# A's queries projected transposed in a gated mix of linear and sliding-window attention on one core: denominators beside the numerators, heads copied by ScalarE and normalised by GpSimd, gate logits on TensorE

## The chip, the cores and the metric

One core of a Trainium2 chip runs the kernel. The metric is device time in microseconds (us), the median of three runs. The core has five engines with a queue of instructions each: TensorE (PE, its weight loads are listed as PEld), VectorE (DVE), ScalarE (ACT), GpSimd (POOL) and SyncE (SP), which issues most DMAs. Matmul results lie in PSUM, the other tiles in SBUF.

## What is computed

Both attentions share the input x of 2048 rows and 1024 columns; there are 32 heads of 32 columns.

```python
def _A_ref(x, wqkv, wo):
    q, k, v = ...                                   # x @ wqkv, split into 32 heads of 32
    phi = lambda t: jnp.where(t > 0, t + 1, jnp.exp(t)) + 1e-6
    pq, pk = phi(q), phi(k)
    kv = jnp.einsum("bhsd,bhse->bhde", pk, v)
    z = jnp.einsum("bhsd->bhd", pk)
    num = jnp.einsum("bhqd,bhde->bhqe", pq, kv)
    den = jnp.einsum("bhqd,bhd->bhq", pq, z)[..., None] + 1e-6
    return merge_heads(num / den) @ wo
def _B_ref(x, wqkv, wo):
    W, dil = 8, 2                                   # a query sees itself and 7 keys, 2 apart
    ...
    attn = _softmax(jnp.where(mask, logits * Dh ** -0.5, -1e9))
    return merge_heads(jnp.einsum("bhsw,bhswd->bhsd", attn, vg)) @ wo
g = _sigmoid((x * gate_w).sum(-1, keepdims=True))
return g * _A_ref(...) + (1 - g) * _B_ref(...)
```

The kernel writes g as e/(1+e) with e = exp(logit) and 1−g as 1/(1+e). So A's normalised heads are multiplied by e, both outputs go into one sum in PSUM, and that sum is multiplied by 1/(1+e) (the tile `omg`; e is `el`).

## The kernel before

**Tiles.** Because the window steps by two, even and odd rows of x never meet in B. The kernel splits them into two parities p of 1024 rows, each of eight tiles of 128 rows; a *pair* is a tile and the one four further on in the same parity. x lies transposed in SBUF (xT), columns on partitions.

**Projections.** A `Group` makes a 2×2 block of 128×512 (or, for column groups, 512-row) results with seven products instead of eight (m1 to m7, a Strassen form), four 128×512 matmuls each. For this, sums of x (`xsums`) and of the weights (`Weights.sums`) are made beforehand. Products accumulate in four PSUM banks X0, Y0, X1, Y1. Three intermediate results per group are copied out by ACT (`save`, L266); of the four final blocks one is written by ACT (L237) and three are added by DVE (L239). The last products m3 and m4 of a group run inside the next group. A *row group* has rows of x on partitions of its result, a *column group* has weight columns there, so that its result is transposed.

**Attention as filler.** After each product `side(rate)` draws steps from a queue of generators: score steps and numerator steps of B, and the KV sums of A. B works on items (four heads of each half, nn = 0 to 3, times parity p); each has ten score steps (L513, then exp on ACT L520 and the mask on DVE L522) and nine numerator steps (L532). A numerator step makes 114 rows of eight heads with 33 columns, the last of which is the softmax denominator, since V carries a column of ones. DVE takes its reciprocal (L535) and multiplies straight out of PSUM (L537), and SP stores the tile (L542) in OB_d.

**Stages.** x and B's value weights are loaded and transposed; the first two pairs are projected in the plain way; `xsums` of all pairs; B's values for pairs 2 to 7 (a DRAM tensor V_d); B's keys and queries nn = 0; `gate` for 16 tiles (x rows loaded again, a DVE multiply-and-reduce L227, exp on ACT); A's keys and values as row groups, with phi (ACT L397, DVE L398 and L399), the sum of phi(k) on GpSimd (L418) and KV on PE (L437); B's nn = 1 lies between them and nn = 2, 3 around A's queries. A's queries are row groups (`qa_group`): phi, then per tile GpSimd multiplies by the sum of phi(k) (L486), DVE reduces over each head (L488), L491 to L493 turn this into e/den, GpSimd scales (L495) and SP stores PQ_d (L496). Meanwhile `kv_end` multiplies KV into A's output weights (L465). At the end 16 output tiles: two transposing DMAs each (L651, L653) and 32 matmuls (L659, L661).

**Order.** Every engine works its queue in order, and a scheduler has fixed that order when the kernel was built. Pools (`bufs`) decide when a tile is free for the next writer. SP carries all loads and stores of the middle and the end in one queue.

Of the kernel before, what the change touches and what calls it, by code (L numbers as in the profile page):

```python
# [14 lines left out]
P = 128  # L15
QB = 114
NBLK = 9
EPS = 1e-6


@with_exitstack
def kernel(
# [31 lines left out]
    PQ_d = [dram.tile([P, D], BF16, name=f"PQ_d{t}") for t in range(16)]  # L54

    chainp = ctx.enter_context(tc.tile_pool(name="chainp", bufs=5))
    tring = ctx.enter_context(tc.tile_pool(name="tring", bufs=4))
    ering = ctx.enter_context(tc.tile_pool(name="ering", bufs=4))
    smallp = ctx.enter_context(tc.tile_pool(name="smallp", bufs=4))
    obp = ctx.enter_context(tc.tile_pool(name="obp", bufs=4))  # L60
# [6 lines left out]
    ph1 = ExitStack()  # L67
    xp = ph1.enter_context(tc.tile_pool(name="xp", bufs=1))
    kqp = ph1.enter_context(tc.tile_pool(name="kqp", bufs=2))
    vwp = ph1.enter_context(tc.tile_pool(name="vwp", bufs=2))  # L70
    ptp = ph1.enter_context(tc.tile_pool(name="ptp", bufs=1))
    prodp = ph1.enter_context(tc.tile_pool(name="prodp", bufs=2))
# [7 lines left out]
    S4 = xp.tile([P, 4, 2, 512], FP16, name="S4")  # L80

# [5 lines left out]
    def xsums(p, c0, c1):  # L87
        sl = slice(c0 * P, c1 * P)
# [3 lines left out]
        s3 = xT.bitcast(FP16)[:, 0:4, p, 1, sl]  # L92
        tt = nc.vector.tensor_tensor
        tt(out=s1, in0=a21, in1=a22, op=ALU.add)
        tt(out=s2, in0=s1, in1=a11, op=ALU.subtract)
        tt(out=s3, in0=a11, in1=a21, op=ALU.subtract)
        tt(out=s4, in0=a12, in1=s2, op=ALU.subtract)

    class XOp:


        def get(self, m, kc, p, sl):
            if m == 1:
                return xT[:, kc, p, 0, sl]
            if m == 2:
                return xT[:, 4 + kc, p, 0, sl]
            if m == 4:
                return xT[:, 4 + kc, p, 1, sl]
            if m == 7:
                return xT.bitcast(FP16)[:, kc, p, 1, sl]  # L110
            return {3: S4, 5: S1, 6: S2}[m][:, kc, p, sl]

    xop = XOp()

    class Weights:

        def __init__(self, n, W, T, eng, parts=1):
            self.n, self.W, self.T, self.eng = n, W, T, eng  # L120
            self.W16 = W.bitcast(FP16)

        def sums(self, lo=0, hi=4):
            n, W, T, tt = self.n, self.W, self.T, self.eng.tensor_tensor
            b11, b12 = W[:, lo:hi, 0:n], W[:, lo:hi, n:2 * n]
            b21, b22 = W[:, 4 + lo:4 + hi, 0:n], W[:, 4 + lo:4 + hi, n:2 * n]
            t3 = self.W16[:, lo:hi, n:2 * n]
            t1, t2, t4 = T[:, 0, lo:hi, :], T[:, 1, lo:hi, :], T[:, 2, lo:hi, :]
            tt(out=t1, in0=b12, in1=b11, op=ALU.subtract)
            tt(out=t3, in0=b22, in1=b12, op=ALU.subtract)  # L130
            tt(out=t2, in0=b22, in1=t1, op=ALU.subtract)
            tt(out=t4, in0=b21, in1=t2, op=ALU.subtract)

        def get(self, m, kc, sl):
            n = self.n
            lo, hi = sl.start, sl.stop
            if m == 1:
                return self.W[:, kc, lo:hi]
            if m == 2:
                return self.W[:, 4 + kc, lo:hi]  # L140
            if m == 3:
                return self.W[:, 4 + kc, n + lo:n + hi]
            if m == 7:
                return self.W16[:, kc, n + lo:n + hi]
            return self.T[:, {5: 0, 6: 1, 4: 2}[m], kc, lo:hi]

    def row_weights(src, col0, eng, dq, quarters=True):
# [3 lines left out]
        for j in range(2):  # L151
            for i in range(2):
                dq.dma_start(out=W[:, 4 * i:4 * i + 4, 512 * j:512 * j + 512],
                             in_=view[:, 4 * i:4 * i + 4, col0 + 512 * j:col0 + 512 * j + 512])
        return Weights(512, W, T, eng)

    def col_weights(src, col0, nn, eng, dq):
# [3 lines left out]
        for j in range(2):  # L161
            c0 = col0 + 512 * j + nn * P
            dq.dma_start(out=W[:, :, j * P:(j + 1) * P], in_=view[:, :, c0:c0 + P])
        return Weights(P, W, T, eng)
# [4 lines left out]
    wvB = None  # L169
    xt_load(0)  # L170
    W = wp.tile([P, 8, D], BF16, name="W", tag="W")
    T = tp.tile([P, 3, 4, 512], FP16, name="T", tag="T")
    bview = B_wqkv.rearrange("(k p) n -> p k n", p=P)

    def vb_load(dq, i, j):
        dq.dma_start(out=W[:, 4 * i:4 * i + 4, 512 * j:512 * j + 512],
                     in_=bview[:, 4 * i:4 * i + 4, 2 * D + 512 * j:2 * D + 512 * j + 512])
    vb_load(nc.scalar, 0, 0)
    vb_load(nc.scalar, 1, 0)
    xt_load(4)  # L180
    vb_load(nc.scalar, 0, 1)
    vb_load(nc.scalar, 1, 1)
    for t in (1, 5, 2, 6, 3, 7):
        xt_load(t)
    wvB = Weights(512, W, T, nc.vector)
    for t in (8, 12, 9, 13, 10, 14, 11, 15):
        xt_load(t)
# [15 lines left out]
    bd = consts.tile([P, P], F32, name="bd")  # L203
    nc.gpsimd.memset(bd[:], 0.0)
    for i in range(4):
        nc.gpsimd.memset(bd[32 * i:32 * i + 32, 32 * i:32 * i + 32], 1.0)
    ones = consts.tile([P, P], F32, name="ones")
    nc.gpsimd.memset(ones[:], 1.0)
    gw_row = prodp.tile([P, D], BF16, name="gw_row", tag="prod")
    nc.sync.dma_start(out=gw_row[:], in_=gate_w.partition_broadcast(P))  # L210
    el = consts.tile([P, 16], F32, name="el")
    omg = consts.tile([P, 16], F32, name="omg")
    zacc = consts.tile([P, D], F32, name="zacc")
    KVacc = consts.tile([P, D], F32, name="KVacc")
    KVb = consts.tile([P, 8, P], BF16, name="KVb")
# [5 lines left out]

    def gate(t):
        xt = tring.tile([P, D], BF16, name="xrow", tag="t")
        nc.sync.dma_start(out=xt[:], in_=xrows(t))
        junk = ering.tile([P, D], BF16, name="gjunk", tag="e")
        dot = smallp.tile([P, 1], F32, name="gdot", tag="gdot")
        nc.vector.tensor_tensor_reduce(out=junk[:], in0=xt[:], in1=gw_row[:], scale=1.0, scalar=0.0,  # L227
                                       op0=ALU.mult, op1=ALU.add, accum_out=dot[:])
        nc.scalar.activation(out=el[:, t:t + 1], in_=dot[:], func=ACT.Exp)
        nc.vector.tensor_scalar(out=omg[:, t:t + 1], in0=el[:, t:t + 1], scalar1=1.0, scalar2=None,  # L230
                                op0=ALU.add)
        nc.vector.reciprocal(out=omg[:, t:t + 1], in_=omg[:, t:t + 1])
# [10 lines left out]
    class Group:  # L243
# [3 lines left out]
        def __init__(self, final, done=None):  # L247
            self.final, self.done = final, done
# [3 lines left out]
        def operands(self, m, kc):  # L252
            raise NotImplementedError

        def mm(self, ps, m, start, stop):
            for kc in range(4):
                lhsT, rhs = self.operands(m, kc)
                nc.tensor.matmul(ps[:], lhsT=lhsT, rhs=rhs, start=start and kc == 0,  # L258
# [439 lines left out]
```

## Time and profile before

| quantity | value |
|---|---|
| median of three runs | 604.92 us (603.25 to 605.2) |
| the profiled execution, as timed | 605.71 us |
| its span in the trace | 603.9 us |
| instructions in the trace | 8465 |
| DMA | 56.15 MB, mean 93 GB/s |

The profile gives busy time per engine, a chain of waits from the last instruction back to the first, groups of instructions by source line (`out<-in`, with the partitions and elements), and stretches of the span with the busy time of each engine. The granted clock is TensorE's, 1.0 at full speed. An engine that waits is idle, and what ended the idle time is named behind an arrow. The lines themselves are shown in the prediction.

### The profile page before, as it was taken

What the parts mean: (1) busy time and instruction counts of PE and PEld (TensorE: products, weight loads), DVE (VectorE), ACT (ScalarE), POOL (GpSimd) and SP (SyncE); (2) the same over time, 40 slices, a digit from 0 to 9 for tenths busy, and PEclk for the clock granted to TensorE, in tenths of its full rate; (3) what the DMA queues carried; (4) which work ended last, traced back from release to release, by engine and by line L of the source; (5) the groups of instructions that cost most, each with busy time, mean ns of one, the idle gap of its engine ahead of it and who ended that gap; (6) DMA issues with size and microseconds to landing.
All of it is one profiled execution on the core that took longest, in us unless ns stands there. A gap on an engine that the chain in (4) does not pass through costs nothing.

```text
span 603.9 us, 8465 instructions
## 1 busy us (share of the span) xinstructions
PE 504.1 (83%) x3140; PEld 234.5 (39%) x3194; DVE 371.3 (61%) x648; ACT 225.3 (37%) x347; POOL 215.1 (36%) x156
## 2 busy tenths in 40 slices
PE   7769985889999998979979765694986389999997
PEld 4324431334444444434444322242332244444443
DVE  1643469999777568878454988858488964001100
ACT  1313332455553465525644542254353143100000
POOL 6059348453222056222816775314056500000000
PEclk9969996979999999989979986595797769999999
DMA  9997481700200240027403121103108366554311
GB/s 232 174 246 213 134 264 49 186 22 13 49 9 11 48 88 9 13 49 238 154 21 74 46 68 43 52 8 95 51 14 183 100 133 139 124 114 112 63 44 35
DMA packets 126057, 56.15 MB, mean 93 GB/s; under 512 B 105408, under 2 KB 117696, under 8 KB 126016
## 3 DMA queue, kind: packets, MB, share of 16 engines
q1 hardware_dynamic: 123904, 53.51, 35.9%
q10 hardware_dynamic: 2112, 2.10, 1.2%
q8 instruction: 25, 0.41, 0.3%
q14 instruction: 16, 0.13, 0.1%
HBM read 26.10 MB, written 16.91 MB: 71 GB/s over the span
## 4 chain that ended last, share of the span: by engine, by line
PE 48%; DVE 29%; issue 5%; POOL 5%; ACT 3%; DMA 3%; SPq 0%; another core or an unknown queue 0%; DVEq 0%; ACTq 0%
PE X L258 14%; PE Y L258 12%; PE po L661 9%; PE po L659 8%; DVE eA L399 6%; DVE PT L522 5%; POOL prod L486 4%; DVE gjunk L227 4%; DVE tA L239 2%; DVE tA L398 2%; DVE den L488 2%; PE s L513 2%; ACT PT L520 2%; DMA xrow<-in_A_x_dram 2%; DVE ob L537 1%
## 5 line engine op out<-in xcount | busy, mean ns | idle before, releaser
L520 ACT ACTIVATE PT<-s 128x912 bf16<-128x912 f32 (+1 forms) x80 | 68.6, 857 | 61.5 <-PE o L532 32.4
L522 DVE TENSOR_TENSOR PT<-PT,maskp 128x912 bf16<-128x912 bf16 (+1 forms) x80 | 65.9, 828 | 20.3 <-ACT PT L520 20.0
L258 PEld LDWEIGHTS <-xT 128*128 128x128 bf16 (+1 forms) x480 | 46.0, 100 | 78.6 <-issue 33.6
L258 PE MATMUL Y<-W,xT 128*128 128x512 f16 (+1 forms) x233 | 63.4, 394 | 14.7 <-DVE va L239 9.9
L258 PE MATMUL X<-T,S 128*128 128x512 f16 x240 | 63.8, 388 | 1.3 <-ACT M1s L266 0.8
L659 PE MATMUL po<-WoA,pqT 128*128 128x512 bf16 x249 | 61.8, 388 | 3.4 <-DMA pqT<-PQ_d 2.9
L486 POOL TENSOR_TENSOR prod<-eA,zacc 128x512 f32<-128x512 bf16 x32 | 41.0, 1304 | 64.5 <-DVE eA L399 51.0
L661 PE MATMUL po<-WoB,obT 128*128 128x512 bf16 x249 | 62.6, 386 | 1.5 <-DMA obT<-OB_d 1.1
L665 DVE TENSOR_SCALAR osb<-po,omg 128x512 bf16<-128x512 f32 x16 | 12.0, 750 | 82.5 <-PE po L661 82.4
L418 POOL TENSOR_TENSOR zacc<-zacc,eA 128x1024 f32<-128x1024 f32 x15 | 33.6, 2239 | 69.4 <-DVE eA L399 46.2
L266 ACT COPY U4s<-X 128x512 f32<-128x512 f32 x46 | 26.9, 585 | 78.9 <-PE X L258 76.9
L532 PE MATMUL o<-vw,PT 128*128 128x33 bf16 x576 | 30.1, 184 | 28.4 <-DVE PT L522 21.2
L399 DVE SCALAR_TENSOR_TENSOR eA<-eA,tA 128x1024 bf16<-128x1024 bf16 x32 | 52.4, 1637 | 0.6
L258 PEld LDWEIGHTS <-S 128*128 128x128 f16 x360 | 33.7, 99 | 41.3 <-issue 4.9
L258 PE MATMUL Y<-xT,WS 128*128 128x512 f16 (+1 forms) x124 | 39.9, 450 | 8.6 <-DVE qT L239 3.6
L513 PE MATMUL s<-qT,kT 32*128 32x114 bf16 x576 | 34.4, 234 | 15.0 <-ACT PT L520 12.7
L532 PEld LDWEIGHTS <-PT 128*128 128x128 bf16 x576 | 25.5, 101 | 48.6 <-DVE PT L522 28.7
L663 ACT ACTIVATE osb<-po,omg 128x512 bf16<-128x512 f32 x16 | 11.0, 687 | 83.0 <-PE po L661 82.9
L258 PEld LDWEIGHTS <-WS 128*128 128x128 bf16 (+1 forms) x256 | 25.5, 105 | 40.1 <-issue 18.6
L258 PE MATMUL Y<-T,xT 128*128 128x512 f16 x120 | 32.2, 391 | 7.9 <-DVE tA L239 6.5
L397 ACT ACTIVATE eA<-tA 128x1024 bf16<-128x1024 bf16 x32 | 33.9, 1060 | 11.6 <-DVE tA L239 8.7
L659 PEld LDWEIGHTS <-pqT 128*128 128x128 bf16 x256 | 25.0, 99 | 33.3 <-DMA pqT<-PQ_d 3.1
(93 smaller groups left out, 781.6 us busy)
## 6 DMA issues: line engine op xcount, KB each, us to landing
W<-in_A_wqkv_dram SPq DMA_DIRECT2D x12, 512.0 KB
vw<-V_d SPq DMA_DIRECT2D x72, 66.0 KB
V_d<-va SPq DMA_DIRECT2D x16, 264.0 KB
WS<-in_B_wqkv_dram SPq DMA_DIRECT2D x16, 256.0 KB
xrow<-in_A_x_dram SPq DMA_DIRECT2D x16, 256.0 KB
PQ_d<-eA SPq DMA_DIRECT2D x16, 256.0 KB
out_dram<-osb SPq DMA_DIRECT2D x32, 128.0 KB
OB_d<-ob SPq DMA_DIRECT2D x64, 57.0 KB
```

Source lines behind the costliest of these rows:

```text
L258: nc.tensor.matmul(ps[:], lhsT=lhsT, rhs=rhs, start=start and kc == 0, stop=stop and kc == 3, skip_group_check=True)
L266: nc.scalar.copy(out=s[:], in_=ps[:])
L397: nc.scalar.activation(out=e[:], in_=t[:], func=ACT.Exp)
L399: nc.vector.scalar_tensor_tensor(out=e[:], in0=e[:], scalar=EPS, in1=t[:], op0=ALU.add, op1=ALU.min)
L418: nc.gpsimd.tensor_tensor(out=zacc[:], in0=zacc[:], in1=e[:], op=ALU.add)
L486: nc.gpsimd.tensor_tensor(out=prod[:], in0=pq[:, 512 * h:512 * h + 512], in1=zacc[:, 512 * h:512 * h + 512], op=ALU.mult)
L513: nc.tensor.matmul(s[:, gi, e * QB:(e + 1) * QB], lhsT=kT[32 * g:32 * g + 32, ch, k0:k0 + P], rhs=qT[32 * g:32 * g + 32, ch, q0:q0 + QB], ...
L520: nc.scalar.activation(out=PT[:, :, 0:w], in_=s[:, :, 0:w], func=ACT.Exp, scale=SCALE)
L522: nc.vector.tensor_tensor(out=PT[:, :, 0:w], in0=PT[:, :, 0:w], in1=m[:, None, :].broadcast_to([P, 2, w]), op=ALU.mult)
L532: nc.tensor.matmul(o[:, hh, :], lhsT=pts[g // 2][:, g % 2, e * QB:e * QB + P], rhs=vw[:, b, hh, :], start=True, stop=True)
L659: nc.tensor.matmul(po[:], lhsT=pqT[:, c, :], rhs=W2["Wo"][:, c, hs], start=c == 0, stop=False)
L661: nc.tensor.matmul(po[:], lhsT=obT[:, c, :], rhs=(WoB6[:, c, hs] if c < 6 else WoB2[:, c - 6, hs]), start=False, stop=c == 7)
```

## The change

1. **Gate.** The logit of a tile is eight matmuls of 128×1 on xT (128 in all, into one PSUM tile); exp, +1 and reciprocal are done once for all 16 tiles.
2. **KV with denominators.** A's values also carry a column of ones, so one matmul per chunk of 128 columns makes KV and the sum of phi(k) beside it (33 columns per head). KVz is this, masked to the block diagonal. The sum on GpSimd, `kv_end`'s product into Wo and the DVE reductions go.
3. **A's queries** are column groups, one per (nn, p), so that phi(q) is transposed. Two matmuls of 128×132 per 128 rows then give numerators and denominators of eight heads.
4. **Normalising.** Both A and B copy the heads from PSUM with ACT into an SBUF tile `of` (two blocks), DVE makes the reciprocals there, GpSimd multiplies, SP stores.
5. **Phi** is three DVE operations instead of two; its queries' form works on 128×2×512.
6. **Weight sums** are all on DVE (GpSimd made most of them before). B's weights nn = 3 and A's query weights are loaded once for each parity.
7. **Order.** B's values for pairs 4 to 7 are interleaved with B's first heads, A's keys and values with nn = 1, 2. A's queries run parity by parity, and output tiles 0 to 5 are interleaved with those of the second parity; transposes come three tiles at a time.

```diff
-    def gate(t):
-        xt = tring.tile([P, D], BF16, name="xrow", tag="t")
...
-        nc.vector.tensor_tensor_reduce(out=junk[:], in0=xt[:], in1=gw_row[:], scale=1.0, scalar=0.0,
-                                       op0=ALU.mult, op1=ALU.add, accum_out=dot[:])
+    def gate(t):
...
+        for kc in range(8):
+            nc.tensor.matmul(gps[:, t:t + 1], lhsT=xT[:, kc, p, hf, c * P:(c + 1) * P], rhs=gw[:, kc:kc + 1],
+                             start=kc == 0, stop=kc == 7)
...
-        nc.vector.tensor_scalar(out=t[:], in0=t[:], scalar1=0.0, scalar2=1.0, op0=ALU.max, op1=ALU.add)
-        nc.vector.scalar_tensor_tensor(out=e[:], in0=e[:], scalar=EPS, in1=t[:], op0=ALU.add, op1=ALU.min)
+        nc.vector.tensor_scalar(out=t, in0=t, scalar1=0.0, scalar2=None, op0=ALU.max)
+        nc.vector.tensor_scalar(out=e, in0=e, scalar1=1.0, scalar2=EPS, op0=ALU.min, op1=ALU.add)
+        nc.vector.tensor_tensor(out=e, in0=e, in1=t, op=ALU.add)
...
+    def normalise(of, n, rows, gate_t):
+        rec = smallp.tile([P, 2, 8, 1], F32, name="rec", tag="rec")
+        r = rec[0:rows, 0:n]
+        if gate_t is None:
+            nc.vector.reciprocal(out=r, in_=of[0:rows, 0:n, :, 32:33])
+        else:
+            nc.vector.tensor_scalar(out=r, in0=of[0:rows, 0:n, :, 32:33], scalar1=EPS, scalar2=None, op0=ALU.add)
+            nc.vector.reciprocal(out=r, in_=r)
+            nc.vector.tensor_tensor(out=r, in0=r, in1=el[0:rows, gate_t:gate_t + n][:, :, None, None]
+                                    .broadcast_to([rows, n, 8, 1]), op=ALU.mult)
+        ob = ofp.tile([P, 2, 8, 32], BF16, name="ob", tag="ob")
+        nc.gpsimd.tensor_tensor(out=ob[0:rows, 0:n], in0=of[0:rows, 0:n, :, 0:32], in1=r.broadcast_to([rows, n, 8, 32]),
+                                op=ALU.mult)
...
+    def qa_group(w, nn, p):
...
+        def out(i):
+            for k0 in (0, 2):
+                of = ofp.tile([P, 2, 8, 33], F32, name="of", tag="of")
+                for k in range(2):
+                    o = ps_o.tile([P, 8, 33], F32, name="oA", tag="o")
...
+                        nc.tensor.matmul(o[:, 4 * j:4 * j + 4, :].rearrange("p h e -> p (h e)"),
+                                         lhsT=e[:, j, s0:s0 + P], rhs=KVz[:, nn + 4 * j, :],
+                                         start=True, stop=True)
+                    nc.scalar.copy(out=of[:, k], in_=o[:])
+                    yield
+                ob = normalise(of, 2, P, 8 * p + 4 * i + k0)
+                for k in range(2):
+                    nc.sync.dma_start(out=cols_of(OA_d[p][i][r0:r0 + P, :], nn), ...)
...
-            nc.vector.reciprocal(out=rec[0:QB], in_=o[0:QB, :, 32:33])
-            nc.vector.tensor_tensor(out=ob[0:QB], in0=o[0:QB, :, 0:32], in1=rec[0:QB].broadcast_to([QB, 8, 32]),
-                                    op=ALU.mult)
+            nc.scalar.copy(out=of[0:QB, e0], in_=o[0:QB])
...
+    run(lambda: q_group(wqB[3], 3, 1), RATE_Q)
+    load_qa(1)
+    run(lambda: qa_group(wqA[0], 0, 1), RATE_O)
+    out_n(0, 1, RATE_O)
...
+    run(lambda: qa_group(wqA[3], 3, 1), RATE_O)
+    out_n(3, 4, RATE_O)
+    flush(RATE_O)
+    out_n(4, 6, 3.0)
+    while queue:
+        step()
+    out_n(6, 16, 0)
```

The rings change with it: `of` and `ob` have three buffers each, the ring of va/vA/tA/osb tiles and that of eA five each instead of four; the transposed keys, queries and phi tiles share four.

What this makes of the queues shows at three places. The first is DVE's queue within A's queries: tA (before) and tq (after) are the raw queries, eA and eq their exp and then phi. Before:

```order
L239 TENSOR_TENSOR tA<-Y,M1s 128x512
L398 TENSOR_SCALAR tA<-tA 128x1024
L239 TENSOR_TENSOR tA<-Y,U2s 128x512
L399 SCALAR_TENSOR_TENSOR eA<-eA,tA 128x1024
L398 TENSOR_SCALAR tA<-tA 128x1024
L399 SCALAR_TENSOR_TENSOR eA<-eA,tA 128x1024
L488 TENSOR_REDUCE den<-prod 128x16 x2
L239 TENSOR_TENSOR tA<-Y,U4s 128x512
L491 TENSOR_SCALAR den<-den 128x32
```

And of the change, where TS are sums of the next weights:

```order
L434 TENSOR_SCALAR rec<-of 128x16
L435 RECIPROCAL rec<-rec 128x16
L436 TENSOR_TENSOR rec<-rec,el 128x16
L377 TENSOR_SCALAR tq<-tq 128x2x512
L378 TENSOR_SCALAR eq<-eq 128x2x512
L214 TENSOR_TENSOR tq<-Y,U2s 128x512
L379 TENSOR_TENSOR eq<-eq,tq 128x2x512
```

In DVE's queue the reductions that waited for GpSimd's products have been replaced by reciprocals that wait for ACT's copies; the additions out of PSUM (L239, now L214) still stand between them.

The second place is SP's queue in the same part, in the second parity. Before:

```order
L542 DMA OB_d_63<-ob 228x1x128
L565 DMA vw<-V_d_61 128x2x132 x9
L496 DMA PQ_d_73<-eA 128x1024
L496 DMA PQ_d_77<-eA 128x1024
L651 DMA_TRANSPOSE pqT<-PQ_d_64 128x8x128
```

And of the change, where WS are weights of a later group:

```order
L469 DMA OA_d_64<-ob 256x1x128 x2
L160 DMA WS<-in_A_wqkv_dram 128x8x128
L469 DMA OA_d_64<-ob 256x1x128 x2
L469 DMA OA_d_65<-ob 256x1x128 x4
L580 DMA_TRANSPOSE inT<-OA_d_64 128x8x128 x3
L523 DMA OB_d_63<-ob 228x1x128 x2
L160 DMA WS<-in_A_wqkv_dram 128x8x128 x2
```

Loads of weights now stand between many small stores and behind them, where one store of 128×1024 per tile stood.

The third place is DVE's queue at the start of the program, where va are the first values of B that DVE adds out of PSUM and S the sums of x. Before:

```order
L95 TENSOR_TENSOR S_130<-S_129,xT 128x4x128
L96 TENSOR_TENSOR xT<-xT 128x4x128
L97 TENSOR_TENSOR S_131<-xT,S_130 128x4x128
L130 TENSOR_TENSOR W<-W 128x4x512
L96 TENSOR_TENSOR xT<-xT 128x4x128
L239 TENSOR_TENSOR va<-Y,M1s 128x16x32
```

And of the change:

```order
L98 TENSOR_TENSOR S_115<-S_114,xT 128x4x128
L99 TENSOR_TENSOR S_116<-xT,S_115 128x4x128
L100 TENSOR_TENSOR xT<-xT 128x4x128 x3
L127 TENSOR_TENSOR TS<-WS 128x512
L128 TENSOR_TENSOR TS<-WS,TS 128x512
L214 TENSOR_TENSOR va<-Y,M1s 128x16x32
```

In both queues the first va stands behind the last sums of x; in the change two sums of the first B head's weights have come between them.

More of the change, by code (lines that the diff above doesn't have):

```diff
@@ L113 @@
[L113 to L145, printed above, removed]
@@ L392, in phi_tiles @@
[L392 to L400 removed]
+    gps = ps_o.tile([P, 16], F32, name="gps", tag="o")
@@ new lines, with load_kq @@
+    wkB, wqB = {}, {}
+    def load_kq(nn):
+        wkB[nn] = col_weights(B_wqkv, D, nn)
+        wqB[nn] = col_weights(B_wqkv, 0, nn)
+        wkB[nn].sums()
+        wqB[nn].sums()
+    vb_classical(0)
+    vb_classical(1)
+    wvB.sums()
+    for pair in (2, 3):
+        for i in range(2):
+            gate(tile_of(pair, i))
+        xsums(pair)
+    for pair in (2, 3):
+        run(lambda: vb_group(pair), 0)
+    load_kq(0)
+    wkA = row_weights(A_wqkv, D)
+    xsums(0)
+    xsums(1)
+    for pair in range(4, 8):
+        for i in range(2):
+            gate(tile_of(pair, i))
+        xsums(pair)
```

636 lines of the change are left out of this document (317 added, 319 removed).

## The prediction

> **What bounds the kernel now.** I first read the page's busy shares and its chain of waits, then the table of busy time by stretch. The columns of the second fence are: start and end, length, busy time and count on PE, PEld, DVE, ACT and POOL, the granted TensorE clock, DMA share, GB/s.
>
> ```profile
> PE 504.1 (83%) x3140; PEld 234.5 (39%) x3194; DVE 371.3 (61%) x648; ACT 225.3 (37%) x347; POOL 215.1 (36%) x156
> ...
> PE 48%; DVE 29%; issue 5%; POOL 5%; ACT 3%; DMA 3%; SPq 0%; another core or an unknown queue 0%; DVEq 0%; ACTq 0%
> ```
>
> ```profile
> 0.00:36.00 36.00, 21.72 (x104) 11.03 (x107) 17.02 (x38) 7.06 (x11) 10.48 (x38) 0.89 1.03 212
> 36.00:72.00 36.00, 35.80 (x151) 15.64 (x154) 10.65 (x16) 12.36 (x22) 26.60 (x22) 0.92 0.64 188
> 72.00:140.00 68.00, 54.20 (x308) 23.21 (x311) 61.33 (x109) 27.48 (x55) 36.41 (x14) 0.87 0.44 126
> 140.00:280.00 140.00, 128.46 (x945) 61.51 (x963) 105.82 (x163) 71.38 (x109) 41.14 (x21) 0.99 0.19 46
> 280.00:320.00 40.00, 35.89 (x228) 17.31 (x228) 23.77 (x47) 19.18 (x32) 18.34 (x5) 0.87 0.37 112
> 320.00:485.00 165.00, 115.67 (x771) 54.07 (x780) 128.23 (x227) 67.24 (x93) 82.11 (x56) 0.81 0.26 66
> 485.00:604.00 119.00, 112.35 (x641) 51.72 (x653) 24.53 (x53) 20.63 (x29) 0.00 (x0) 0.97 0.43 96
> ```
>
> PE is 83% busy, yet it carries only 48% of the chain; VectorE (DVE) has 29%. Busy time at a low clock is stretched, so I multiply PE busy by the clock to get full-clock work. The seven stretches give 19.3, 32.9, 47.2, 127.2, 31.2, 93.7 and 109.0: 460 us, leaving 143 us of the span lost. Half of the loss, 165 − 93.7 = 71 us, lies at 320–485, where A's queries run: PE reaches 57% of full work there, against 127.2/140 = 91% at 140–280. The stretch 72–140 (the gate's reductions) loses 21, the start 17.
>
> **Prices on PE.** In the timeline a row gives start, length and count. The last row is from the chain.
>
> ```profile
> 207.91 1.03 PE L258 MATMUL X<-S,TS 128*128 128x512 f16 x4
> 208.87 0.38 PE L513 MATMUL s<-qT,kT 32*128 32x114 bf16 x8
> 209.18 0.82 PE L258 MATMUL X<-W,xT 128*128 128x512 bf16 x3
> ...
> 165.18 0.36 PE L532 MATMUL o<-vw,PT 128*128 128x33 bf16 x8
> 165.38 1.02 PE L258 MATMUL X<-W,S 128*128 128x512 bf16 x4
> ...
> 154.40 0.62 PE L437 MATMUL kps<-eA,vA 128*128 128x128 bf16 x8
> 154.85 1.03 PE L258 MATMUL X<-T,S 128*128 128x512 f16 x4
> ```
>
> ```profile
> 598.02 1.74 PE po L661 x8
> ```
>
> A 128x512 matmul costs 1.74/8 = 0.217. Starts give the rest: 207.91 to 209.18 is 1.27, less four products (0.87), so a score step is 0.40; a B numerator step is 165.38 − 165.18 = 0.20, or 25 ns a matmul; eight 128x128 matmuls are 0.45, or 56 ns each. PE ends at 599.8 and the span at 603.9, so 4.1 us follow the last matmul.
>
> **The change, engine by engine.** First PE. It gains 128 gate matmuls with one column; no row shows that width, so the ends are 0 (slipped between larger ones) and 56 ns each (the 128-column row); I take the nearest row, the 33-column one: 128 × 0.025 = 3.2 us, bounds 0 and 7. A's numerators add 128 matmuls of 132 columns at 0.057: 7.3 us. Folding KV into Wo goes: 16 matmuls of 512 columns, 3.5 us, and a few for the denominators. PE's work goes from 460 to about 467: the gain cannot come from here.
>
> Now DVE, in groups by line (busy us, mean ns, idle before), then by source (shortest/median/longest).
>
> ```profile
> L227 DVE CUSTOM_DVE_ANT_0 gjunk<-xrow,gw_row 128x1024 bf16<-128x1024 bf16 x16 | 31.5, 1970 | 2.1 <-DMA xrow<-in_A_x_dram 2.0
> L537 DVE TENSOR_TENSOR ob<-o,rec 114x256 bf16<-114x256 f32 x72 | 28.8, 410 | 1.3 <-DMA OB_d<-ob 0.7
> L535 DVE RECIPROCAL rec<-o 114x8 f32<-114x8 f32 x72 | 13.4, 196 | 9.0 <-PE o L532 9.0
> L488 DVE TENSOR_REDUCE den<-prod 128x16 f32<-128x512 f32 x32 | 21.6, 676 | 9.1 <-POOL prod L486 9.1
> L492 DVE RECIPROCAL den<-den 128x32 f32<-128x32 f32 x16 | 5.5, 341 | 0.0
> L398 DVE TENSOR_SCALAR tA<-tA 128x1024 bf16<-128x1024 bf16 x32 | 22.8, 711 | 8.2 <-ACT eA L397 8.1
> L399 DVE SCALAR_TENSOR_TENSOR eA<-eA,tA 128x1024 bf16<-128x1024 bf16 x32 | 52.4, 1637 | 0.6
> L129 DVE TENSOR_TENSOR T<-W 128x2048 f16<-128x2048 bf16 x1 | 1.2, 1218 | 0.0
> L94 DVE TENSOR_TENSOR S<-xT 128x512 f16<-128x512 bf16 x8 | 3.4, 423 | 18.0 <-DMA xT<-in_A_x_dram 18.0
> ```
>
> ```profile
> L398 DVE TENSOR_SCALAR tA<-tA x32: 381/420/2355, 132.5 to 466.2; 128x1024 bf16<-128x1024 bf16 x32
> ...
> L399 DVE SCALAR_TENSOR_TENSOR eA<-eA,tA x32: 1154/1226/2820, 133.4 to 469.4; 128x1024 bf16<-128x1024 bf16 x32
> ...
> L522 DVE TENSOR_TENSOR PT<-PT,maskp x80: 344/626/3866, 99.4 to 505.3; 128x912 bf16<-128x912 bf16 x64, 128x456 bf16<-128x456 bf16 x16
> ...
> L520 ACT ACTIVATE PT<-s x80: 550/930/971, 94.1 to 504.5; 128x912 bf16<-128x912 f32 x64, 128x456 bf16<-128x456 f32 x16
> ...
> L486 POOL TENSOR_TENSOR prod<-eA,zacc x32: 1149/1160/2147, 332.5 to 473.1; 128x512 f32<-128x512 bf16 x32
> ```
>
> Gone from DVE: the gate, 31.5. B's normalising was 28.8 + 13.4 = 42.2; 40 reciprocals stay at about 0.2, so 34 go. Of A's denominators L488 goes with three small operations like L492 (16 × 3 × 0.34 = 16): 38 together. Added: 32 reciprocal triples for A, each 3 × 0.2 = 0.6, 19 in all; and all weight sums, since GpSimd gives them up: 72 of 512 columns at 0.42 and 8 of 2048 at 1.22, 40 in all. Phi: the fused L399 (1.23) becomes a tensor_scalar and a tensor_tensor. The first is like L398's median, 0.42, the second is L522's 0.626 × 1024/912 = 0.70. Three operations take 0.42 + 0.42 + 0.70 = 1.54 against today's means of 0.71 + 1.64 = 2.35: −26 us over 32. If the delays that lift those means above the medians stay, only the medians count, 1.54 against 0.42 + 1.23: −3. Together with Wo's eight copies (−6) and wider KV additions (+2), DVE goes from 371 to about 295 us, or 318 at the other end.
>
> ACT gains 136 copies of 264 elements out of PSUM. L520 rises from 0.55 to 0.93 between 456 and 912 elements per half, 0.83 ns an element of one row, so a copy is about 0.55 − 192 × 0.83/1000 = 0.39: 53 us (at most 0.55 each, 75). With Wo's copies gone ACT stands at about 270. GpSimd loses all its products, sums and scalings and keeps 72 multiplications. L486 (512 columns) prices them at 1.16: 84 us at most, against 215. Eight of them have half the columns, so a little less.
>
> **What stays.** PE's longest stop at the start is this:
>
> ```profile
> 36.04 1.86 PE L258 MATMUL Y<-W,xT 128*128 128x512 f16 x4 [9.94 <-DVE va L239]
> ```
>
> In the new order of DVE the first va addition still stands behind the x sums of all eight pairs. The stop therefore stays, and about half of the gate matmuls lie in it free. I keep 36 us for the start.
>
> **The sum**, stage by stage. From 36 us to the last of A's keys and values PE has 932 projection matmuls (202), 45 score steps (18.1), 45 numerator steps (9.1), KV (7.2) and some gates (1.6): 238 us. With the gate's reductions gone, the whole should run like 140–280: 238/0.91 = 261. Then come the last B heads, A's queries and output tiles 0 to 5: 504 matmuls of 512 columns (344 of projection, 160 of output; 109), scores 10.9, numerators 5.5, A's numerators 7.3: 133 us. What share does PE reach here? No row shows this mixture. Its ends are 57%, where DVE, GpSimd and ACT wait on one another now, and 91%. The product-reduce-scale round between GpSimd and DVE is gone; what is left behind PE is one ACT copy, three tiny DVE operations and one GpSimd multiplication, none of which PE waits for unless a ring of three runs out. But copies, sums of weights just loaded and phi all fall into this stage. I take 80%: 133/0.80 = 166. The remaining 352 output matmuls take 352 × 0.217 = 76, the end 4. Span: 36 + 261 + 166 + 76 + 4 = 543. The profiled run took 605.71 with a span of 603.9, so 1.8 lies around it: 545. That execution lies 0.8 above the median of 604.92, which is within the rounding here.
>
> At 91% in both stages the time is 525; without the stop at the start, some 10 less. At 70% it is 569.
>
> **Rivals.** First, GpSimd's multiplications stop DVE. Today L399 takes up to 2.82 us where its median is 1.23, and over the kernel it loses 52.4 − 32 × 1.226 = 13 us. If every multiplication held DVE up for its whole length, the 47 in the last mixed stage (15 for three items of B, 32 for A) would add 47 × 1.16 = 55 us to DVE there. DVE's own load there is about 107: 128 today, less 36 + 13 for denominators and B's normalising, less 13 for half of phi, plus 19 + 22 for triples and 13 sets of sums. At 162 us and nine tenths busy the stage takes 180 instead of 166, and if half of the other 25 (29 us) shows in the stage before, the time is 545 + 14 + 14 = 573. The Trainium skill, "Perfetto Trace Analysis", section Optimizing Scalar/DVE Operations, says that GpSimd and DVE share an SBUF read port, so that moving work between the two might not help; by that rule this rival decides. The trace agrees only in part: L399's median lies near its shortest, 1.15, although GpSimd is busy 36% of the span.
>
> Second, **slower than before**: the chain behind A's queries takes the place of the old one. Each half of a group ends in two `of` tiles that need ScalarE, DVE, GpSimd and two stores each on SP, with three `of` and three `ob` in the ring, while the next weights queue on SP behind those stores.
>
> ```profile
> L542 SPq DMA_DIRECT2D OB_d<-ob x72: 626/757/973, 110.7 to 508.5; - x72
> ```
>
> ```profile
> SPq L542 <- DVE ob L537: 113.2, 30, 16.3
> ```
>
> SP already waits 113 us at such stores, up to 16.3 at once, and one issue takes 0.76. If the next weights come late behind them in most groups, PE falls to the 57% of today: 133/0.57 = 233, span 610, time 612. It decides from the point where the stage lasts over 229 us, a share under 58%. Against it: 64 stores for A and 27 for B are 69 us of issues in a stage of 166, and weights are asked for a group ahead.
>
> Third, the change does not do what it says before A's queries: sums put on DVE and copies put on ACT take the gate's place there, and that stage keeps the 84% that 36–320 has today (32.9 + 47.2 + 127.2 + 31.2 = 238.5 of 284). Then it takes 283, and with A's queries at 70% (190) the time is 36 + 283 + 190 + 76 + 4 + 2 = 591.
>
> **Chances.** The forecast's own family, 518 to 569: 0.66. GpSimd against DVE, near 573: 0.14. The first stage unimproved, near 591: 0.07. Slower, the late weights: 0.07. Better than 518 (both stages over 91%, the start shorter): 0.04. No change: 0.02. The range 518 to 598 holds the first three, 0.87; it takes in the open ends of phi (23 us on DVE) and of the copies (22 us on ACT), which lie off PE. A measurement of this kernel can tell about 0.3% from no change. Faster 0.91, same 0.02, slower 0.07.
>
> **What would show it.** Right: PE's busy share times clock near 0.91 before A's queries and 0.8 in them; the last pure output stretch 76 to 80 us long; L377 and L378 at 0.42, L379 near 0.7, the ACT copies near 0.39, GpSimd's multiplications at 1.16; the first va addition still near 35 us. Wrong: DVE operations with means far above their medians wherever GpSimd is busy; PE idle before the first product of a query group with a weight load or its sums as the releaser; SP waits longer than 10 us at L469 or L523.

## The result and the profile after

The changed kernel took **524.61 us** (median of four runs, 522.7 to 528.21) against 605.06 for the kernel before in the same session: a ratio of 0.868, with a 95% interval of 0.863 to 0.873. The forecast was 545, its range 518 to 598. The profiled execution took 528.21 with a span of 526.4, so again 1.8 us lie around the span; it is the longest of the four.

The page's shares and its chain of waits, of the changed kernel:

```profile
PE 491.1 (93%) x3430; PEld 231.4 (44%) x3430; DVE 295.8 (56%) x610; ACT 258.6 (49%) x458; POOL 91.8 (17%) x136
...
PE 75%; DVE 8%; SPq 7%; ACT 4%; DMA 2%; issue 2%; POOL 1%; POOLq 0%; DVEq 0%; ACTq 0%
```

PE now carries 75% of the chain instead of 48%, DVE 8% instead of 29%. The stretches, cut where the forecast's stages end (columns as before: length, busy time on PE, PEld, DVE, ACT, POOL, clock):

```profile
0.00:39.50 39.50, 24.85 (x171) 13.52 (x172) 16.74 (x37) 7.15 (x11) 11.81 (x40) 0.93 1.06 211
39.50:284.00 244.50, 243.25 (x1845) 114.98 (x1845) 155.48 (x286) 144.65 (x245) 30.10 (x49) 0.99 0.31 80
284.00:445.30 161.30, 145.73 (x1059) 68.08 (x1057) 113.16 (x273) 98.78 (x191) 46.72 (x45) 0.96 0.55 119
445.30:526.40 81.10, 77.28 (x359) 34.81 (x356) 10.47 (x17) 7.99 (x13) 3.13 (x3) 1.00 0.42 96
```

In the second stretch PE is busy 243 of 244.5 us at a clock of 0.99: hardly anything is left to gain there. Between the start and that stretch stands the stop that the change left in place:

```profile
39.53 1.86 PE L230 MATMUL Y<-T3v,xT 128*128 128x512 f16 x4 [10.13 <-DVE va L214]
```

What PE waited for shows the difference best. The first fence is the kernel before at 320 to 485 us (total, times, longest), the second the changed kernel at 284 to 445:

```profile
PE o L532 <- DVE PT L522: 15.8, 9, 6.5
PE Y L258 <- DVE tA L239: 11.9, 8, 3.0
PE s L513 <- ACT PT L520: 9.1, 13, 1.0
PE o L532 <- DVE ob L537: 6.3, 6, 2.0
```

```profile
PE X L230 <- DMA WS<-in_A_wqkv_dram: 3.4, 2, 2.3
PE oA L461 <- ACT of L464: 2.7, 8, 0.5
PE o L513 <- DVE PT L503: 2.0, 2, 1.7
PE s L494 <- ACT PT L501: 1.7, 3, 0.7
```

Before, PE lost 43 us in these four waits, 34 of them to DVE and 9 to ACT's exp. None names GpSimd or A's denominators; they name the masks of B, the additions of the projections and the normalising of B. But a wait names only the last instruction that PE needed, not what stood ahead of it in its queue. In the kernel before, PE waited 3.62 us for one of these masks:

```profile
376.43 0.53 PE L532 MATMUL o<-vw,PT 128*128 128x33 bf16 x12 [3.62 <-DVE PT L522]
```

Meanwhile DVE did this:

```profile
372.80 0.69 DVE L488 TENSOR_REDUCE den<-prod 128x16 f32<-128x512 f32 x1 [0.72 <-POOL prod L486]
373.92 0.69 DVE L488 TENSOR_REDUCE den<-prod 128x16 f32<-128x512 f32 x1 [0.43 <-POOL prod L486]
374.52 1.22 DVE L399 SCALAR_TENSOR_TENSOR eA<-eA,tA 128x1024 bf16<-128x1024 bf16 x1
375.65 0.17 DVE L491 TENSOR_SCALAR den<-den 128x32 f32<-128x32 f32 x1
375.74 0.63 DVE L522 TENSOR_TENSOR PT<-PT,maskp 128x912 bf16<-128x912 bf16 x1
```

The mask stood behind two reductions that each waited for GpSimd's product. Added up over DVE's timeline, in the 34 us that PE waited for DVE in this stretch DVE worked 12 us at the denominators' own lines (L488 to L493) and was idle for 4; the rest went into masks, phi and additions. After the change DVE is on time.

### The profile page after: what moved, and what is told of

It reads as the page before. It is cut to its first block, busy times and chain, and to the rows that moved or that the text cites. A ratio compares the mean times of both kernels' runs of the same rounds, so it can differ in the third digit from the quotient of the medians.

```text
span 526.4 us, 9142 instructions
## 1 busy us (share of the span) xinstructions
PE 491.1 (93%) x3430; PEld 231.4 (44%) x3430; DVE 295.8 (56%) x610; ACT 258.6 (49%) x458; POOL 91.8 (17%) x136
## 4 chain that ended last, share of the span: by engine, by line
PE 75%; DVE 8%; SPq 7%; ACT 4%; DMA 2%; issue 2%; POOL 1%; POOLq 0%; DVEq 0%; ACTq 0%
PE X L230 26%; PE po L592 21%; PE Y L230 20%; SPq L87 6%; PE s L494 4%; PE o L513 2%; PE kps L408 2%; DMA WS<-in_A_wqkv_dram 1%; ACT PT L501 1%; DVE eq L379 1%; ACT eA L376 1%; DMA WS<-in_B_wqkv_dram 1%; DVE tq L214 1%; POOL ob L439 1%; ACT eq L376 1%
## 5 line engine op out<-in xcount | busy, mean ns | idle before, releaser
L439 POOL TENSOR_TENSOR ob<-of,rec 114x512 bf16<-114x512 f32 (+2 forms) x72 | 75.0, 1047 | 272.1 <-DVE rec L432 156.9
L592 PEld LDWEIGHTS <-inT 128*128 128x128 bf16 x512 | 49.7, 99 | 58.1 <-issue 3.4
L503 DVE TENSOR_TENSOR PT<-PT,maskp 128x912 bf16<-128x912 bf16 (+1 forms) x80 | 50.4, 630 | 27.9 <-ACT PT L501 27.7
L592 PE MATMUL po<-WoA,inT 128*128 128x512 bf16 x256 | 62.3, 387 | 0.0
L592 PE MATMUL po<-WoB,inT 128*128 128x512 bf16 x256 | 61.5, 382 | 0.0
L230 PE MATMUL Y<-xT,WS 128*128 128x512 bf16 (+1 forms) x192 | 52.3, 384 | 1.0 <-DVE kT L214 1.0
L230 PE MATMUL X<-S,TS 128*128 128x512 f16 x192 | 50.6, 379 | 2.1 <-ACT U2s L238 1.2
L230 PE MATMUL Y<-W,xT 128*128 128x512 bf16 (+1 forms) x152 | 39.4, 380 | 0.0
L238 ACT COPY M1s<-X 128x512 f32<-128x512 f32 x46 | 27.0, 588 | 18.5 <-PE X L230 17.4
L238 ACT COPY U2s<-X 128x512 f32<-128x512 f32 x46 | 27.0, 586 | 12.9 <-PE X L230 12.9
L515 ACT COPY of<-o 114x264 f32<-114x264 f32 x72 | 27.5, 385 | 10.1 <-PE o L513 9.6
```

Of the source, the lines that this page charges most:

```text
L238: nc.scalar.copy(out=s[:], in_=ps[:])
L439: nc.gpsimd.tensor_tensor(out=ob[0:rows, 0:n], in0=of[0:rows, 0:n, :, 0:32], in1=r.broadcast_to([rows, n, 8, 32]), op=ALU.mult)
L503: nc.vector.tensor_tensor(out=PT[:, :, 0:w], in0=PT[:, :, 0:w], in1=m[:, None, :].broadcast_to([P, 2, w]), op=ALU.mult)
L515: nc.scalar.copy(out=of[0:QB, e0], in_=o[0:QB])
L592: nc.tensor.matmul(po[:], lhsT=w[:, 2 * k + n, c, :], rhs=Wo[key][:, c, hs], start=n == 0 and c == 0, stop=n == 1 and c == 7)
```

## The experiments

Each was timed in three rounds beside the kernel before; four of them shared its runs each time. Differences are given in microseconds of the ratio to before times 605. For the changed kernel itself that ratio is 0.868.

### Is it the denominators, and is it the wait for them or the load?

`b_noden`, the kernel before without A's denominators (it leaves out GpSimd's products, DVE's reductions and GpSimd's scaling):

```diff
                 pq = phi(ts[i])
-                den = smallp.tile([P, H], F32, name="den", tag="den")
-                for h in range(2):
...
-                nc.gpsimd.tensor_tensor(out=v, in0=v, in1=den[:, :, None].broadcast_to([P, H, 32]), op=ALU.mult)
                 nc.sync.dma_start(out=PQ_d[t][:], in_=pq[:])
```

> The kernel before without A's denominators: GpSimd's products, DVE's reductions and GpSimd's scaling are left out, and phi of A's queries is stored as it is, so the output is not the reference's. Theory (the rounds between GpSimd and DVE in A's queries are what the change took away): PE's share at 320 to 485 us rises from 57% to 80% or more, 40 to 50 us less, about 560. Rival (GpSimd's load slows DVE wherever it runs): GpSimd loses 72 us of work, at 15% of that some 11 us less, about 594. Rival (the gain is the new order of the work): under 5 us, about 600.

Measured: 565.6 us, 0.932 of before (0.928 to 0.935), 41 us less. That is what the theory said. But the run takes away the waits, 41 us of DVE's work (L488 to L493) and GpSimd's load all at once, so a second run put the load back. Its edit against `b_noden`:

```diff
...
                 nc.sync.dma_start(out=PQ_d[t][:], in_=pq[:])
+                for h in range(2):
+                    prod = prodp.tile([P, 512], F32, name="prod", tag="prod")
+                    nc.gpsimd.tensor_tensor(out=prod[:], in0=pq[:, 512 * h:512 * h + 512],
+                                            in1=zacc[:, 512 * h:512 * h + 512], op=ALU.mult)
+                v = pq[:].rearrange("p (h e) -> p h e", e=32)
+                nc.gpsimd.tensor_tensor(out=junk[:].rearrange("p (h e) -> p h e", e=32), in0=v,
+                                        in1=el[:, 0:1][:, :, None].broadcast_to([P, H, 32]), op=ALU.mult)
```

> The kernel before without A's denominators, as in the first run (565.6 us, 0.932 of before), but with GpSimd's three multiplications per tile still done, into tiles that nobody reads; DVE's reductions and A's scaling are left out, so the output is not the reference's. It tells the wait apart from the load. If DVE and PE lost their time by waiting for GpSimd's products, the time stays at 0.93 to 0.945 of before, 565 to 573. If GpSimd's work itself slows DVE (as doubling it did in the changed kernel: 77 us more on GpSimd made DVE 33 us busier and the kernel 29 us longer), most of the gain is lost: 0.965 or more, over 585.

Measured: 593.8 us, 0.980 (0.975 to 0.985). Of the 41 us, 28 are back, though nothing waits for these products. The shares of the two runs, first without GpSimd's products, then with them:

```profile
PE 491.8 (88%) x3140; PEld 230.5 (41%) x3194; DVE 320.4 (57%) x568; ACT 224.4 (40%) x347; POOL 141.8 (25%) x108
```

```profile
PE 510.2 (86%) x3194; PEld 233.9 (39%) x3194; DVE 359.1 (60%) x568; ACT 224.7 (38%) x347; POOL 229.0 (38%) x156
```

GpSimd is 87 us busier, and DVE, with the same 568 instructions, 39 us: 0.44 for each. The fused operation of phi in the same two runs (shortest/median/longest):

```profile
L399 DVE SCALAR_TENSOR_TENSOR eA<-eA,tA x32: 1208/1224/2819, 133.2 to 426.3; 128x1024 bf16<-128x1024 bf16 x32
```

```profile
L399 DVE SCALAR_TENSOR_TENSOR eA<-eA,tA x32: 1207/1580/2818, 134.6 to 459.0; 128x1024 bf16<-128x1024 bf16 x32
```

The shortest and the longest stay, the median moves: more of the 32 fall together with a GpSimd operation. So GpSimd's work alone, with nothing waiting for it, can cost 28 us. That is not the load's share of the 41, for put back in this way it holds DVE more than it did before: B's masks take 65.9 us in the kernel before, 57.1 without the denominators and 73.7 with the products back; L399 takes 52.4, 45.5 and 57.7. In the kernel before, the denominators cost DVE three things: 41 us of its own work, 9 us of waiting for products (the idle time of L488), and some 17 us by which its masks and phi were longer than in `b_noden`. Waiting is the smallest of the three; how the 41 us of the kernel's time divide among them these runs do not separate.

### Doubling GpSimd's work in the changed kernel

`a_double`:

```diff
         nc.gpsimd.tensor_tensor(out=ob[0:rows, 0:n], in0=of[0:rows, 0:n, :, 0:32], in1=r.broadcast_to([rows, n, 8, 32]),
                                 op=ALU.mult)
+        nc.gpsimd.tensor_tensor(out=ob[0:rows, 0:n], in0=of[0:rows, 0:n, :, 0:32], in1=r.broadcast_to([rows, n, 8, 32]),
+                                op=ALU.mult)
```

> The changed kernel with every GpSimd multiplication done twice into the same tile: GpSimd 92 to about 167 us busy. Theory (GpSimd is off the path, and its work leaves DVE alone): within 4 us of the changed kernel, 522 to 529, with the medians and means of DVE's operations unchanged. Rival (GpSimd's work holds DVE up): DVE's busy time rises by a tenth or more of the 75 us added, the time by 8 us or more, over 532.

Measured: 553.3 us, 0.912 (0.908 to 0.916), some 27 us more. The theory, that GpSimd's work leaves DVE alone, falls with this run.

```profile
PE 491.1 (89%) x3371; PEld 232.9 (42%) x3430; DVE 328.6 (60%) x610; ACT 259.2 (47%) x458; POOL 169.2 (31%) x208
```

GpSimd +77, DVE +33, at the same 610 instructions: 0.42 for each. But not all of the 27 us need come from there. Each `of` tile is also free a microsecond later, and the copies that fill it wait:

```profile
ACT of L466 <- POOL ob L441: 19.8, 14, 3.9
```

```profile
PE oA L463 <- ACT of L466: 9.5, 10, 2.9
```

In the changed kernel these waits are 5.5 and 2.7 us. This run does not separate the two ways. How one operation is held shows in its timeline:

```profile
109.46 1.11 POOL L441 TENSOR_TENSOR ob<-of,rec 114x512 bf16<-114x512 f32 x1
109.58 1.27 DVE L378 TENSOR_SCALAR eA<-eA 128x1024 bf16<-128x1024 bf16 x1
...
110.77 0.68 DVE L214 TENSOR_TENSOR tA<-Y,U2s 128x512 bf16<-128x512 f32 x1
```

GpSimd's multiplication starts at 109.46 and ends at 110.57. DVE's tensor_scalar starts 0.12 us later and ends at 110.85: 0.28 after GpSimd's end, 1.27 long where 0.42 is its median in the changed kernel. It was held for nearly the whole of GpSimd's instruction. The addition out of PSUM behind it takes its normal 0.68. The same two kinds in the changed kernel:

```profile
L378 DVE TENSOR_SCALAR eA<-eA x16: 411/418/1272, 110.2 to 278.1; 128x1024 bf16<-128x1024 bf16 x16
```

```profile
L214 DVE TENSOR_TENSOR tA<-Y,U2s x8: 676/684/684, 110.5 to 275.9; 128x512 bf16<-128x512 f32 x8
```

The operation between SBUF tiles goes up to three times its median; the addition from PSUM never does. In `a_double`, 32 of the 138 such additions ran beside GpSimd for more than 0.3 us, and none of them took more than 0.70. The Trainium skill, "SBUF — State Buffer", section Who interferes with whom, says that a DVE instruction in a two-port mode and GpSimd lock each other out for a whole instruction, whoever issues first, and that a DVE instruction with at most one SBUF input outside these modes does not contend. These rows agree with both halves, though the profile does not name the mode.

### The multiplications on DVE instead

`a_ob_dve`:

```diff
-        nc.gpsimd.tensor_tensor(out=ob[0:rows, 0:n], in0=of[0:rows, 0:n, :, 0:32], in1=r.broadcast_to([rows, n, 8, 32]),
+        nc.vector.tensor_tensor(out=ob[0:rows, 0:n], in0=of[0:rows, 0:n, :, 0:32], in1=r.broadcast_to([rows, n, 8, 32]),
```

> The changed kernel with the 72 multiplications on DVE instead of GpSimd (from the same SBUF tile). Theory (giving them to GpSimd is a gain, since DVE is late in A's queries): DVE about 335 us busy, 3 to 12 us more, 528 to 537. Rival (the two engines share a port, so that moving work between them gains nothing): 520 to 526, with shorter DVE operations elsewhere.

Measured: 520.8 us, 0.858 (0.854 to 0.862), some 6 us less. The sign of the theory was wrong.

```profile
PE 483.5 (93%) x3371; PEld 231.4 (45%) x3430; DVE 313.4 (60%) x682; ACT 258.7 (50%) x458; POOL 17.5 (3%) x64
```

```profile
L439 DVE TENSOR_TENSOR ob<-of,rec 114x512 bf16<-114x512 f32 (+2 forms) x72 | 46.9, 656 | 2.2 <-DMA OA_d<-ob 0.9 <-issue 0.3
```

DVE does 46.9 us of multiplications more and is only 17.6 us busier, since its other work shrinks by 29: 0.39 for each of the 74 us that GpSimd lost. The multiplication itself takes 0.66 on DVE and 1.05 on GpSimd. Giving it to GpSimd saves DVE 47 us and costs it 29.

`a_b_psum` did the same for B alone, in the form of before (reciprocal and multiplication out of PSUM on DVE, no ScalarE copy):

```diff
-            nc.scalar.copy(out=of[0:QB, e0], in_=o[0:QB])
+            nc.vector.reciprocal(out=rec[0:QB], in_=o[0:QB, :, 32:33])
+            nc.vector.tensor_tensor(out=of[0:QB, e0], in0=o[0:QB, :, 0:32], in1=rec[0:QB].broadcast_to([QB, 8, 32]),
+                                    op=ALU.mult)
...
```

> The changed kernel with B's heads normalised on DVE straight out of PSUM, as before; A's stay with ScalarE and GpSimd. DVE gains 72 times 0.61 less 9 us of reciprocals, 35 us, and by 0.4 for each of GpSimd's 42 us gets 17 back; ACT loses 28 us of copies. If DVE's busy time decides: 3 to 10 us more, 528 to 535. If GpSimd's quiet in the stages before A's queries is worth more: 520 to 526.

Measured: 520.9 us, 0.862 (0.857 to 0.867), some 4 us less by the middle, with intervals that still overlap (0.863 to 0.873). It does not cost anything, which the first guess said it would; that it gains is not shown.

### The weight sums back on GpSimd

`a_sums_pool`:

```diff
         def __init__(self, n, W, T, T3=None):
             self.n, self.W, self.T = n, W, T
+            self.eng = nc.gpsimd if T3 is None else nc.vector
...
-            n, W, T, tt = self.n, self.W, self.T, nc.vector.tensor_tensor
+            n, W, T, tt = self.n, self.W, self.T, self.eng.tensor_tensor
```

> The changed kernel with the weight sums back on GpSimd (all but those of B's values): 72 sums of 512 columns at about 1.38 us and 8 of 2048 at 4.06, by the rows of the kernel before, 132 us more on GpSimd. If a microsecond on GpSimd costs DVE about 0.4, as the doubled multiplications showed, DVE loses 42 us of sums and gains some 53: it is no less busy, and the time rises by 10 to 30 us, to 535 to 555 (sums that come late add to it). If only the waits matter and the sums are early enough: 522 to 530.

Measured: 569.6 us, 0.941 (0.935 to 0.946), some 44 us more: more than any other part that was undone in the changed kernel, and more than either theory said.

```profile
PE 503.0 (89%) x3430; PEld 235.4 (42%) x3430; DVE 316.8 (56%) x530; ACT 258.4 (46%) x458; POOL 214.2 (38%) x216
```

DVE gives up 80 instructions and is 21 us *busier*. The run also brings stops, two of which are:

```profile
59.45 1.86 PE L231 MATMUL Y<-xT,WS 128*128 128x512 f16 x4 [9.33 <-DVE kT L215]
```

```profile
127.08 1.87 PE L231 MATMUL X<-T,S 128*128 128x512 f16 x4 [6.34 <-POOL T L129]
```

The second is a sum that came late, so the 44 us are load and lateness together; how much of each was not separated.

### The gate

`b_gate_pe` is the kernel before with the gate's logits on TensorE, `a_gate_dve` the changed kernel with them back on DVE. The edit of the first:

```diff
-        nc.vector.tensor_tensor_reduce(out=junk[:], in0=xt[:], in1=gw_row[:], scale=1.0, scalar=0.0,
-                                       op0=ALU.mult, op1=ALU.add, accum_out=dot[:])
...
+            nc.tensor.matmul(gps[:, t:t + 1], lhsT=xT[:, kc, p, hf, c * P:(c + 1) * P], rhs=gw[:, kc:kc + 1],
+                             start=kc == 0, stop=kc == 7)
```

> The kernel before with only the gate's logits on TensorE. Theory: the stretch 72 to 140 us, which loses 21 us to the reductions on DVE, gets most of it back: 12 to 20 us less, 585 to 593. Rival (the reductions lay beside work that waits anyway): under 4 us, 601 or more.

Measured: 593.6 us, 0.978 (0.971 to 0.985), 13 us less.

> The changed kernel with the gate's reductions back on DVE, x rows loaded again, before A's first keys. Theory (their 31 us of DVE work cost what the same move gave in the kernel before, 13 us): 532 to 540. Rival (with GpSimd quiet DVE has room in that stretch): DVE is some 55% busy there, the reductions fit in, 526 or less.

Measured: 539.5 us, 0.889 (0.885 to 0.894), some 13 us more. The gate is worth about the same in both kernels. In `a_gate_dve` the reductions take 19.3 us, against 31.5 in the kernel before; this row is followed by the two stops of PE that they bring:

```profile
L328 DVE CUSTOM_DVE_ANT_0 gjunk<-xrow,KVacc 128x1024 bf16<-128x1024 bf16 x16 | 19.3, 1212 | 0.0
```

```profile
127.91 1.86 PE L228 MATMUL X<-W,xT 128*128 128x512 bf16 x4 [12.06 <-ACT vA L210]
...
134.51 1.87 PE L228 MATMUL Y<-W,xT 128*128 128x512 f16 x4 [4.75 <-DVE vA L212]
```

The rival had argued from DVE's mean load. But the reductions stand in one block in DVE's queue, and what PE needs lies behind them: the addition of the second stop directly, the ACT copy of the first behind the exps that ACT's queue has for each reduction.

### Phi and the order

`a_phi2` puts the fused operation back:

```diff
-        nc.vector.tensor_scalar(out=t, in0=t, scalar1=0.0, scalar2=None, op0=ALU.max)
-        nc.vector.tensor_scalar(out=e, in0=e, scalar1=1.0, scalar2=EPS, op0=ALU.min, op1=ALU.add)
-        nc.vector.tensor_tensor(out=e, in0=e, in1=t, op=ALU.add)
+        nc.vector.tensor_scalar(out=t, in0=t, scalar1=0.0, scalar2=1.0, op0=ALU.max, op1=ALU.add)
+        nc.vector.scalar_tensor_tensor(out=e, in0=e, scalar=EPS, in1=t, op0=ALU.add, op1=ALU.min)
```

> The changed kernel with phi in two operations, as before (the fused one at 1.23 us in place of two at 0.42 and 0.68). If the form of phi is worth what the medians say, DVE gains 32 times 0.13, 4 us, and the time 0 to 4 us, to 524 to 529. If the fused form suffers more from GpSimd (its mean was 0.41 above its median before), 530 or more.

Measured: 532.1 us, 0.879 (0.875 to 0.883), some 6 us more, although DVE's busy time hardly moves (297.2 against 295.8). It is more than the medians account for; why was not found. PE's waits for weight sums (L128) grow from 0.9 to 4.1 us, which is part of it at most.

`a_late_out` moved the code of the first six output tiles behind all query groups.

> The changed kernel with all 16 output tiles behind the last query group, none between. The first parity's query groups, which have no output tiles among them, lose 25 us at 320 to 400 us with DVE about 90% busy. If the output tiles between the second parity's groups are what keeps PE busy there, the time rises by 12 to 25 us, to 537 to 550. If the order does not matter, since the waits are DVE's alone: within 4 us, 521 to 529.

Measured: 529.0 us, 0.873 (0.868 to 0.878), no difference that the intervals show. But the scheduler put the tiles between the groups all the same; their first matmul in that run:

```profile
397.29 1.24 PE L592 MATMUL po<-WoA,inT 128*128 128x512 bf16 x5
```

In the changed kernel it starts at 384.4. So this run says nothing about what the interleaving is worth.

### The stop at the start, and a faster version

`a_start` leaves the work as it is and fixes DVE's order in the first 45 us (`first` and `second` are the last additions of va in groups 2 and 3):

```diff
-    for pair in (2, 3):
-        run(lambda: vb_group(pair), 0)
-    load_kq(0)
-    wkA = row_weights(A_wqkv, D)
-    xsums(0)
-    xsums(1)
+    with tc.issue_after(first):
+        xsums(0)
+        xsums(1)
+    with tc.issue_after(second):
+        load_kq(0)
+        wkA = row_weights(A_wqkv, D)
...
-    wkA.sums()
+    with tc.issue_after(last["add"].ins):
+        wkA.sums()
```

> The changed kernel with another order on DVE in its first 45 us: the sums of x for pairs 0, 1 and 4 to 7 and the sums of the first head's weights stand behind the first additions of va. If PE's stop of 10.1 us there comes from DVE's order alone, it goes, and the time falls by 7 to 10 us, to 514 to 518 (0.85 to 0.857 of before). If what PE needs next (weights of the first head, x of the second parity) arrives late anyway, the stop only moves: 2 us or less.

Measured: 518.9 us, 0.855 (0.852 to 0.858), some 8 us less. The first addition of va, which stood at 38.79 us, now comes as soon as its product is there:

```profile
28.12 0.69 DVE L216 TENSOR_TENSOR va<-Y,M1s 128x512 bf16<-128x512 f32 x1 [1.50 <-PE Y L232]
```

`a_best` is `a_start` with the multiplications on DVE.

> Both: the new order at the start and the 72 multiplications on DVE. If the two gains add up (6 to 7 us from the multiplications, 7 to 10 from the start): 508 to 512, 0.84 to 0.847 of before. If they overlap: 515 or more.

Measured: **512.8 us**, 0.846 (0.842 to 0.849), some 14 us under the changed kernel: the two gains add up. PE is then 96% busy.

```profile
PE 488.4 (96%) x3430; PEld 231.5 (45%) x3430; DVE 312.2 (61%) x682; ACT 258.7 (51%) x458; POOL 17.5 (3%) x64
```

## Why the prediction came out as it did

**The time** was in the range, and the sign right; the forecast was 20 us too long. The sum against the changed kernel's profiled execution: start 36, measured 39.5; the stage up to A's values 261, measured 244.5; A's queries 166, measured 161.3; output 76, measured 77.3; end 4, measured 3.8 (526.4 less 522.6, where the chain's last matmuls end). Nearly the whole miss is the second term. It was made by dividing 238 us of PE work by the 91% of the best stretch before; PE reached 238/244.5 = 97%. So the 91% was no property of the mixture. What had lowered it was not tested by itself; that GpSimd was busy 41 of 140 us there and 30 of 244.5 in the changed kernel would fit. For A's queries PE reached 133/161.3 = 82%, close to the 80% of the forecast. That is in part luck, since the 80% was picked between two far ends.

**The work on PE** came out as priced where it can be seen alone: the output's 352 matmuls within 1.3 us. The gate's and A's numerators cannot be told apart in the stages' length.

**DVE's total** of 295 was met (295.8), but not for the reasons given. By `a_ob_dve` some 29 us of the 295.8 are time in which DVE was held by GpSimd; without these DVE's own work would be 267. The agreement is luck. The sum had left the delays of the masks as they were (L522 fell from 65.9 to 50.4 as L503), took out all of phi's, and priced the 32 triples at 19 where the three lines (L434 to L436) show 27.

**The weakest step** is the reason given for the stage of A's queries: "The product-reduce-scale round between GpSimd and DVE is gone". The round is gone, and it did stand ahead of what PE needed. But waiting in it was a small part of its cost on DVE: 9 us of idle time, beside 41 us of DVE's own work and some 17 us that the load added to masks and phi. What GpSimd's load takes from DVE had no term of its own in the stage's sum, and `b_noden_pool` shows that it alone can cost the kernel 28 us.

**The first rival** was mis-sized and mis-aimed. It named the right mechanism, but as a danger of the 84 us that the change gives to GpSimd, not as a gain from the 123 that it takes away. It reckoned with up to 84 us of holding; `a_ob_dve` shows 29. It was given little weight because L399's median lay near its shortest. A median does not show this: most operations are untouched and a few are held for up to a whole GpSimd instruction, so the cost shows in the mean. Over three pairs of runs a microsecond on GpSimd cost DVE 0.39 to 0.44. Two other pairs lie outside: 0.23 between the kernel before and `b_noden` (17 us of masks and phi for 73), where much of GpSimd's work waited for DVE in turn, and 0.5 in `a_sums_pool` (21 us and the 41 of the sums that DVE gave up, L127 to L130, for 122). From 0.23 to 0.44, the change took 28 to 54 us off DVE through GpSimd alone (an estimate), of the 75 by which DVE's busy time fell. The sentence of the Trainium skill in "Perfetto Trace Analysis", section Optimizing Scalar/DVE Operations, that moving work between these two engines might not help, agrees with `a_ob_dve`, and more strongly with `a_sums_pool`.

**What stays** was right: the stop at the start stayed, at 10.1 us. The prediction put it at some 10; `a_start` gained 8 by taking it away.

**The second rival**, weights late behind stores, did not come true, although its sign, a wait of SP longer than 10 us at L523, was seen. SP waited for A's normalised tiles little, and for B's much, without PE following (total, times, longest):

```profile
SPq L523 <- POOL ob L439: 88.4, 27, 14.7
...
SPq L469 <- POOL ob L439: 12.1, 8, 3.8
```

Two waits of PE for A's query weights, 3.4 us together, are all that is seen of it. **The third**, a first stage that gains nothing, was the opposite of what happened there.

**By parts.** Undone one at a time in the changed kernel: weight sums 44 us, gate 13, phi 6; GpSimd's multiplications cost 6 to keep. Taken alone in the kernel before: denominators 41, gate 13. They come from two different kernels and do not add up to the 80. ScalarE's copies for B, tried together with where B is normalised, and the interleaving of output tiles have no value that these runs show, and the transposed projection of A's queries with its numerators was not undone by itself.

## What to carry to other kernels

Before work is moved to an idle GpSimd, count what its SBUF work takes from VectorE: here some 0.4 us for each in three pairs of runs, 0.2 to 0.5 in all, so an operation that is 1.6 times as long there gives back most of what it saves at 0.4. Compare means with the shortest times, not medians, and ask which late instruction PE waited for and what stood ahead of it in its queue. An in-order queue can hide a 10 us stop behind loads that arrive late: look at what stands ahead of the first instruction that PE needs.

## What was unexpected of the hardware

A DVE tensor_scalar of 128x1024 took 1.27 us instead of 0.42 beside one GpSimd multiplication of 1.11, ending 0.28 after it. Additions that read PSUM kept to a median of 0.69 and at most 0.70 in the runs with 17 and with 169 us of GpSimd alike. And moving 80 operations from DVE to GpSimd left DVE 21 us busier.
